# A second batch's first transform stage: sums and differences by GpSimd, all of it ahead of the MLP, with half the products

## The chip, the cores and the metric

The kernel runs on one core of a Trainium2 chip. The metric is the device time of one execution in microseconds (us). A core has five engines that matter here: PE (TensorE, matrix products out of SBUF into PSUM; PEld is its weight load), DVE (VectorE, elementwise work), ACT (ScalarE, elementwise work and copies out of PSUM), POOL (GpSimd, elementwise work within SBUF) and SP (SyncE, which here only issues DMA transfers). Each engine takes the instructions of its queue in order; between engines, semaphores order the work.

## The reference

Eight sequences `x[b]` of 3008 tokens with 256 features are Fourier transformed along the tokens, multiplied by a complex 256 x 256 matrix, biased, soft-thresholded, and transformed back. The result, 24064 tokens, goes through a two-layer MLP of width 2048. All is float32.

```python
X = np.fft.rfft(x, axis=1)
Yr = Xr @ w_r - Xi @ w_i + b_r
Yi = Xr @ w_i + Xi @ w_r + b_i
Yr = np.sign(Yr) * np.maximum(np.abs(Yr) - 0.01, 0.0)
Yi = np.sign(Yi) * np.maximum(np.abs(Yi) - 0.01, 0.0)
y = np.fft.irfft(Yr + 1j * Yi, n=3008, axis=1)
h = y.reshape(24064, 256) @ moe_w_in
out = np.maximum(0.01 * h, h) @ moe_w_out
```

## The kernel before

The length 3008 is split as 47 x 64, so that the transform is a 47-point stage, then a 64-point stage, with no twiddle factors between. The host only reorders the rows of x: for each of 24 frequencies of the 47-point stage it lays out the rows n and 47 - n as two arrays, called here xa and xb, each of 120 partitions.

**First stage, `fwd(b)`.** Of each batch seven column blocks c (six of 512 columns, the last, c = 6, of 256) are loaded (`load`, line 222). Since the 47-point transform of a real sequence needs xa + xb for its cosine part and xa - xb for its sine part, the first batch (b = 0) forms both on DVE (`fold`, line 240) and multiplies the sum by the cosine matrix `fa0` and the difference by the sine matrix `fa1`. Batches 2 to 7 do the same with `fold` on GpSimd, beside the MLP. The second batch (b = 1) is different: `stage_a1` (line 271) takes xa and xb as they are, and for each of the two parts h adds two products, xa by `fa{h}` and xb by `fa0` (cosine) or `fa2` (sine), where `fa2` is `fa1` times -1, made once at line 680. ACT copies each result out of PSUM (line 280) over the input, and SP stores it into a DRAM buffer, `u_dram` (line 281).

**Middle stage, `mid(b)`.** For each of 12 frequency pairs j: load u from `u_dram` (line 329), the 64-point stage (`stage_b`, line 343), the product with the complex matrix (`proj`, lines 375 and following: three real products; DVE adds at line 388, thresholds at 391 and 392; ACT writes the scaled result `zf` at 396 and 400), and the 64-point stage back (`stage_g`, line 414), whose result is stored to `v_dram`. For the first batch all this runs before the MLP, in plain float32, beside the conversion of `w_in` (`convert_win`, lines 131 to 172) from int64 views of float64 into pairs of reduced float32 numbers (`hi`, `lo`) on ACT and DVE. For later batches it is threaded between the MLP's steps.

**Last stage and MLP.** `v_load` (line 459) and `inverse` (line 480) make 470 columns of y at a time; `forms` (lines 505 to 513) makes the seven operands of a Strassen product; then the MLP runs over 47 chunks of 512 tokens with eight steps q each: `moe_a` and `moe_b` (products at line 92, elementwise work at 542 to 563), `moe_o` (line 576). The second weight is converted one piece per step beside the first chunk (`load_wout`, lines 186 to 202).

**Order.** The program is issued in the order of the main part (lines 648 to 739), and a planner that keeps its own times for each instruction then orders the queue of each engine; `tc.issue_after` keeps an instruction from being placed ahead of another one. The second batch's `fwd(1)` is the stream `fp`: its seven loads are issued between steps 5 and 11 of the first middle stage (line 702), `fp.to(0.69)` (line 706) issues `stage_a1` for blocks 0, 1, 2, 3 and 6, and the blocks 4 and 5 are issued inside the MLP loop at its steps 2 and 4 (line 726). `stage_a1` is held behind the eleventh `stage_g` (line 276).

**Buffers.** Tiles share slots by tag. The second batch's inputs `xin` take the tags yc, yc, gf, gh, yl, yh, gh (line 214), which the MLP's own tiles use afterwards. In PSUM, the blocks 4 and 5 use tag psf, the others psh; the MLP's output products use pso.

Of the kernel before, what the change touches and what calls it, by code (L numbers as in the profile page):

```python
# [8 lines left out]
F32 = mybir.dt.float32  # L9
# [12 lines left out]
PA = NK1 * NG  # L22
# [8 lines left out]
def spectral_mlp_kernel(  # L31
# [18 lines left out]
    D = w_r.shape[0]  # L50
# [13 lines left out]
    sb = ctx.enter_context(tc.tile_pool(name="sb", bufs=2))  # L64
# [4 lines left out]
    def bank(tag, bufs):  # L69
        return ps.tile([P, 512], F32, name=tag, tag=tag, bufs=bufs)  # L70

    def products(dst, pairs):

        terms = []
        for l, r in pairs:
            terms += [(l[0], r[0]), (l[0], r[1]), (l[1], r[0])] if len(l) == 2 else [(l[0], r[0])]
        for i, (a, b) in enumerate(terms):
            last = nc.tensor.matmul(dst, a, b, start=(i == 0), stop=(i == len(terms) - 1))  # L78
        return last
# [18 lines left out]
    consts = {}  # L98
# [117 lines left out]
    def fwd(b):  # L216
# [5 lines left out]
        def load(c):  # L222
            cols = slice(2 * c * D, min(2 * c + 2, NS) * D)
            n = cols.stop - cols.start
            if b < NPRE:
                tag, bufs = (XT, XT1)[b][c]
                x2 = sb.tile([PA, 2, 2 * D], F32, name="xin", tag=tag, bufs=bufs)
                x_t[c] = [x2[:, h, :n] for h in range(2)]
            else:
                x_t[c] = [  # L230
                    sb.tile([PA, 2 * D], F32, name=f"xin{h}", tag="uv"[h], bufs=3 - h)[:, :n] for h in range(2)
                ]
            for h, t in enumerate(x_t[c]):
                if b == 0:
                    (act if h else sync).dma_start(t, x[b, h, :, cols])
                else:
                    with tc.issue_after(reads[-1].ins):
                        sync.dma_start(t, x[b, h, :, cols])
# [19 lines left out]
        def stage_a(c, h):  # L258
# [9 lines left out]
            if b == 0:  # L268
                written.append(st)

        def stage_a1(c):

            n = x_t[c][0].shape[1]
            pas = [(bank("psf", 2) if c in (4, 5) else bank("psh", 4))[:PA, :n] for _ in range(2)]
            for h in range(2):
                with tc.issue_after(turning[NPAIR - 2].ins):
                    products(pas[h], [
                        (consts[f"fa{h}32"], (x_t[c][0],)), (consts[f"fa{2 * h}32"], (x_t[c][1],))])
            for h in range(2):
                act.copy(x_t[c][h], pas[h])  # L280
                sync.dma_start(uv[h, :, 2 * c * D:2 * c * D + n], x_t[c][h])

        if b == 1:
            for c in range(NX):
                load(c)
                yield 0
            for c in (0, 1, 2, 3, 6, 4, 5):
                stage_a1(c)
                yield 6 * x_t[c][0].shape[1]
            return  # L290
# [354 lines left out]
    FWD = NS * 6 * D  # L645


    fa32 = sb.tile([PA, 3, PA], F32, name="fa32", tag="xi", bufs=1)
    for h in range(2):
        sync.dma_start(fa32[:, h], fa[h])  # L650
    for h in range(3):
# [25 lines left out]
    act.copy(bz[:1], brow[:1])  # L677
    act.copy(bz[32:33], brow[32:33])
    dve.tensor_sub(bz[32:33], brow[32:33], bz[32:33].bitcast(F32))
    act.mul(fa32[:, 2], fa32[:, 1], -1.0)  # L680
    convert_win(0)
    with tc.issue_after(turned[0].ins):
        split_consts()
# [19 lines left out]
        if i == 13:  # L703
            next(wout)
    m0.finish()
    fp.to(0.69)
    for p in due[0]:
        v_load(p)
    for eh in range(NH):
# [133 lines left out]
```

## Time and profile before

| | |
|---|---|
| median of 3 runs | 2600.41 us (2598.28 to 2602.9) |
| profiled execution, own time | 2600.34 us |
| its span, first to last instruction | 2598.6 us |
| PE busy | 2537.5 us, 98% of the span |
| DVE busy | 1897.1 us, 73% |
| ACT busy | 1668.5 us, 64% |
| POOL busy | 229.6 us, 9% |

All times within the span count from its start. A table by stretches has a row for each: its bounds, its length, and for each engine the busy time in it and, as (x..), how many instructions; then the clock that PE was granted as a share of full speed, the mean busy share of the 16 DMA engines, and the GB/s they moved. A timeline row has start, length, engine, line, operation, what it writes and reads, shapes, and how many in a row are merged (x4); in brackets is the engine's idle time just before, and what ended it. A row of a group has the number of instructions, their busy time, the mean in ns, and the idle time before them. A row "min/median/max" gives the lengths of one in ns. Engine names with a q (SPq) are the engine's sequencer, which issues DMA transfers. The last row of the page's DMA part gives the size of one transfer in KB and the median us from issue to landing.

### The profile page before, as it was taken

Reading aid. Unit: us, or ns where it says so; the run is one execution under the profiler, and the core shown is the slowest. Engines: PE = TensorE matmul, PEld = TensorE weight load, DVE = VectorE, ACT = ScalarE, POOL = GpSimd, SP = SyncE. Lnnn points to the kernel's source line nnn. Section 1 sums busy time; section 2 is a strip of 40 time slices with the busy share of each in tenths; the row PEclk is TensorE's granted clock in tenths of the full one; section 3 lists DMA queues with packets and bytes.
Section 4 is the critical chain, followed back from the end, with each engine's and each line's share of the span. In section 5 each row is a group of like instructions: output and inputs, shape, how many; then the busy total and the mean of one; then the engine's idle time right before and its main releaser. Section 6 shows DMA issues by size and latency. Waiting matters only on the chain.

```text
span 2598.6 us, 42643 instructions
## 1 busy us (share of the span) xinstructions
PE 2537.5 (98%) x16300; PEld 2281.5 (88%) x16300; DVE 1897.1 (73%) x3403; ACT 1668.5 (64%) x3174; POOL 229.6 (9%) x180
## 2 busy tenths in 40 slices
PE   5999999999999999999999999999999999999999
PEld 4689888999889998899988999889998889999998
DVE  7687786776777778777786777877777777767675
ACT  5766665776556666567665666566666667655564
POOL 0001121100110001100021000210002000000000
PEclk8999999999999999999999999999999999999999
DMA  8621132111221113211132111321113221101000
GB/s 259 179 85 50 48 89 72 54 47 48 82 78 49 45 41 90 75 55 51 33 97 68 49 49 37 104 67 49 49 36 101 64 58 48 44 17 32 9 17 17
DMA packets 119912, 165.13 MB, mean 64 GB/s; under 512 B 13601, under 2 KB 69917, under 8 KB 119709
## 3 DMA queue, kind: packets, MB, share of 16 engines
q1 hardware_dynamic: 79120, 115.55, 14.6%
q10 hardware_dynamic: 40589, 46.87, 7.1%
q8 instruction: 128, 2.10, 0.4%
q14 instruction: 75, 0.61, 0.1%
HBM read 86.60 MB, written 75.76 MB: 62 GB/s over the span
## 4 chain that ended last, share of the span: by engine, by line
PE 89%; DVE 3%; DMA 2%; ACT 1%; issue 0%; ACTq 0%; SPq 0%; DVEq 0%
PE pso L576 38%; PE psh L92 34%; PE psf L78 11%; PE psf L480 3%; PE psf L343 3%; DMA u<-u_dram 1%; DMA u_dram<-xin 1%; DVE yl L506 0%; DVE gl L563 0%; DMA raw<-w_out_dram 0%; DVE gf L557 0%; ACT gh L561 0%; DVE yt L511 0%; ACT gf L559 0%; DVE yc L512 0%
## 5 line engine op out<-in xcount | busy, mean ns | idle before, releaser
L92 PE MATMUL psh<-yh,win_hi 128*128 128x256 f32 x2632 | 752.3, 286 | 13.8 <-DVE gf L546 10.6
L92 PE MATMUL psh<-yl,win_hi 128*128 128x256 f32 x2632 | 738.3, 280 | 0.6 <-DVE yl L506 0.5
L92 PE MATMUL psh<-yh,win_lo 128*128 128x256 f32 x2632 | 737.9, 280 | 0.0
L576 PE MATMUL pso<-gh,wout_hi 128*128 128x512 f32 x1504 | 593.9, 395 | 0.0
L576 PE MATMUL pso<-gl,wout_hi 128*128 128x512 f32 x1504 | 591.1, 393 | 0.5 <-DVE gl L563 0.5
L576 PE MATMUL pso<-gh,wout_lo 128*128 128x512 f32 x1504 | 590.4, 393 | 0.0
L563 DVE TENSOR_TENSOR gl<-gf,gh 128x1024 fp32r<-128x1024 f32 x376 | 471.8, 1255 | 92.7 <-ACT gh L561 90.6
L92 PEld LDWEIGHTS psh<-yh,win_hi 128*128 128x128 f32 x2632 | 497.0, 189 | 30.7 <-DVE gf L546 15.4
L92 PEld LDWEIGHTS psh<-yl,win_hi 128*128 128x128 f32 x2632 | 497.0, 189 | 12.5 <-DVE yl L506 1.0
L92 PEld LDWEIGHTS psh<-yh,win_lo 128*128 128x128 f32 x2632 | 496.6, 189 | 0.2
L557 DVE TENSOR_TENSOR gf<-psh,u 128x512 f32<-128x512 f32 x376 | 259.1, 689 | 256.3 <-PE psh L92 255.1
L561 ACT CAST gh<-gf 128x1024 fp32r<-128x1024 f32 x376 | 396.4, 1054 | 7.1
L559 ACT ACTIVATE gf<-gf 128x768 f32<-128x768 f32 x376 | 320.0, 851 | 49.5 <-DVE gf L557 47.7
L576 PEld LDWEIGHTS pso<-gl,wout_hi 128*128 128x128 f32 x1504 | 282.5, 188 | 62.9 <-DVE gl L563 1.0
L576 PEld LDWEIGHTS pso<-gh,wout_hi 128*128 128x128 f32 x1504 | 283.1, 188 | 46.9 <-ACT gh L561 0.4
L576 PEld LDWEIGHTS pso<-gh,wout_lo 128*128 128x128 f32 x1504 | 282.9, 188 | 44.9
L556 ACT ACTIVATE gf<-psh 128x256 f32<-128x256 f32 x376 | 145.5, 387 | 266.6 <-PE psh L92 246.9
L542 ACT COPY p<-psh 128x256 f32<-128x256 f32 x376 | 140.1, 373 | 220.2 <-PE psh L92 219.1
L379 POOL TENSOR_TENSOR kb<-bias,kc 128x512 f32<-128x512 f32 x84 | 119.0, 1417 | 1530.6 <-ACT kc L376 1409.6
L543 DVE TENSOR_TENSOR u<-psh,p 128x256 f32<-128x256 f32 x376 | 158.6, 422 | 105.8 <-ACT p L542 103.5
L545 DVE TENSOR_TENSOR gf<-psh,u 128x256 f32<-128x256 f32 x376 | 159.3, 424 | 29.7 <-PE psh L92 2.0
L546 DVE TENSOR_TENSOR gf<-psh,gf 128x256 f32<-128x256 f32 x376 | 159.1, 423 | 9.0
(134 smaller groups left out, 3253.2 us busy)
## 6 DMA issues: line engine op xcount, KB each, us to landing
u<-u_dram SPq DMA_DIRECT2D x192, 128.0 KB, 2.7
v_dram<-v ACTq DMA_DIRECT2D x192, 128.0 KB, 2.4
out_dram<-ob SPq DMA_DIRECT2D x94, 256.0 KB, 2.1
vin<-v_dram SPq DMA_DIRECT2D x96, 240.0 KB, 3.5
xin<-x_dram SPq DMA_DIRECT2D x90, 240.0 KB, 3.0
u_dram<-xin ACTq DMA_DIRECT2D x72, 240.0 KB, 2.4
u_dram<-xin SPq DMA_DIRECT2D x24, 240.0 KB, 3.9
raw<-w_out_dram SPq DMA_DIRECT2D x8, 512.0 KB, 5.0
```

The source lines that it names most:

```text
L78: last = nc.tensor.matmul(dst, a, b, start=(i == 0), stop=(i == len(terms) - 1))
L92: mlp[:] = [nc.tensor.matmul(dst, a, b, start=start and i == 0, stop=i == 2, skip_group_check=True)]
L542: act.copy(p1, b1[:, lo])
L543: dve.tensor_add(u2, b1[:, hi], p1)
L545: dve.tensor_add(g[:, 3], b2[:, hi], u2)
L546: dve.tensor_add(g[:, 3], b2[:, lo], g[:, 3])
L556: act.activation(g[:, 0], b1[:, lo], AF.Prelu, alpha=SLOPE)
L557: dve.tensor_add(g[:, 1:3], b2.rearrange("p (k n) -> p k n", k=2), u2.unsqueeze(1).broadcast_to([P, 2, HT]))
L559: act.activation(g[:, 1:4], g[:, 1:4], AF.Prelu, alpha=SLOPE)
L561: cp = act.copy(gh, g)
L563: parted[:] = [cp, dve.tensor_sub(gl, g, gh.bitcast(F32))]
L576: mlp[:] = [nc.tensor.matmul(po, a[:, f, s], r[:, i], start=(f == 0 and j == 0), stop=(f == NF - 1 and j == 2),)]
```

## The change

1. `fold1(c)` is new: for the second batch, GpSimd adds and subtracts xa and xb of each block. The sum goes to a spare half tile, the difference over xa. The first spare is a third part of block 4's tile, which is made that much larger; after each block its xb becomes the spare of the next one, in the order 0, 1, 2, 3, 6, 4, 5.
2. `stage_a1` then needs one product for each part instead of two: the sum by `fa0`, the difference by `fa1`. The third matrix `fa2` and the ACT instruction that made it go.
3. The blocks 4 and 5 are no longer held back for the MLP loop: `fp.finish()` issues all folds and all seven blocks ahead of it. In PSUM they use the tag pso instead of psf.

```diff
             if b < NPRE:
                 tag, bufs = (XT, XT1)[b][c]
-                x2 = sb.tile([PA, 2, 2 * D], F32, name="xin", tag=tag, bufs=bufs)
+                spare = b == 1 and c == 4
+                x2 = sb.tile([PA, 3 if spare else 2, 2 * D], F32, name="xin", tag=tag, bufs=bufs)
                 x_t[c] = [x2[:, h, :n] for h in range(2)]
+                if b == 1:
+                    s_t[c] = x2[:, 1]
+                if spare:
+                    s_t[-1] = x2[:, 2]
...
+        def fold1(c):
+
+            xa, xb = x_t[c]
+            n = xa.shape[1]
+            xs = s_t[-1][:, :n]
+            s_t[-1] = s_t.pop(c)
+            pool.tensor_add(xs, xa, xb)
+            pool.tensor_sub(xa, xa, xb)
+            x_t[c] = [xs, xa]
+
         def stage_a1(c):
 
             n = x_t[c][0].shape[1]
-            pas = [(bank("psf", 2) if c in (4, 5) else bank("psh", 4))[:PA, :n] for _ in range(2)]
+            pas = [(bank("pso", 2) if c in (4, 5) else bank("psh", 4))[:PA, :n] for _ in range(2)]
             for h in range(2):
                 with tc.issue_after(turning[NPAIR - 2].ins):
-                    products(pas[h], [
-                        (consts[f"fa{h}32"], (x_t[c][0],)), (consts[f"fa{2 * h}32"], (x_t[c][1],))])
+                    products(pas[h], [(consts[f"fa{h}32"], (x_t[c][h],))])
...
             for c in range(NX):
                 load(c)
                 yield 0
+            for c in (0, 1, 2, 3, 6, 4, 5):
+                fold1(c)
             for c in (0, 1, 2, 3, 6, 4, 5):
                 stage_a1(c)
...
-    fa32 = sb.tile([PA, 3, PA], F32, name="fa32", tag="xi", bufs=1)
+    fa32 = sb.tile([PA, 2, PA], F32, name="fa32", tag="xi", bufs=1)
...
-    act.mul(fa32[:, 2], fa32[:, 1], -1.0)
...
     m0.finish()
-    fp.to(0.69)
+    fp.finish()
...
-        if i in (2, 4):
-            with tc.issue_after(parted[0].ins), tc.issue_after(parted[1].ins):
-                next(fp.gen)
```

More of the change, by code (lines that the diff above doesn't have):

```diff
@@ L645, in spectral_mlp_kernel @@
     FWD = NS * 6 * D
-    fa32 = sb.tile([PA, 3, PA], F32, name="fa32", tag="xi", bufs=1)
+    fa32 = sb.tile([PA, 2, PA], F32, name="fa32", tag="xi", bufs=1)
     for h in range(2):
         sync.dma_start(fa32[:, h], fa[h])
-    for h in range(3):
+    for h in range(2):
         consts[f"fa{h}32"] = (fa32[:, h],)
```

## The prediction

> **What bounds the kernel now.** I read the share of each engine and the chain that ended last first, then a table by stretches of the first 200 us, because every line of the change acts before 150 us.
>
> ```profile
> PE 2537.5 (98%) x16300; PEld 2281.5 (88%) x16300; DVE 1897.1 (73%) x3403; ACT 1668.5 (64%) x3174; POOL 229.6 (9%) x180
> PE 89%; DVE 3%; DMA 2%; ACT 1%; issue 0%; ACTq 0%; SPq 0%; DVEq 0%
> ```
>
> ```profile
> core 0: us, PE busy (x) PEld busy (x) DVE busy (x) ACT busy (x) POOL busy (x), PEclk, DMA share, GB/s
> 58.00:65.00 7.00, 6.36 (x35) 4.93 (x34) 6.87 (x15) 6.46 (x13) 0.00 (x0) 1.00 0.83 266
> 65.00:76.00 11.00, 10.56 (x54) 8.18 (x53) 9.22 (x15) 10.23 (x21) 0.00 (x0) 1.00 0.96 278
> 76.00:85.00 9.00, 9.00 (x48) 7.35 (x47) 8.04 (x17) 7.94 (x18) 0.00 (x0) 1.00 0.52 160
> 85.00:93.00 8.00, 8.00 (x44) 6.65 (x43) 5.09 (x8) 7.74 (x16) 0.00 (x0) 1.00 0.27 66
> 93.00:104.50 11.50, 7.91 (x28) 4.63 (x27) 4.93 (x9) 6.84 (x16) 0.30 (x1) 0.97 0.37 88
> 104.50:116.00 11.50, 11.50 (x31) 5.46 (x30) 6.64 (x12) 4.30 (x7) 0.00 (x0) 0.88 0.73 199
> 116.00:129.00 13.00, 12.87 (x55) 7.87 (x54) 6.83 (x17) 10.81 (x25) 0.00 (x0) 1.00 0.77 239
> 129.00:149.50 20.50, 17.91 (x95) 13.98 (x94) 18.59 (x36) 12.04 (x23) 0.00 (x0) 0.92 0.41 120
> 149.50:168.50 19.00, 16.73 (x106) 14.74 (x104) 18.87 (x41) 15.21 (x32) 0.00 (x0) 1.00 0.33 99
> 168.50:200.00 31.50, 31.44 (x208) 28.86 (x209) 24.43 (x45) 19.83 (x36) 2.58 (x2) 1.00 0.17 51
> ```
>
> Over the whole span TensorE is the chain (89%). From 168.5 us on it is full (31.44 of 31.50), so there a microsecond of start is a microsecond of end. The change, however, sits earlier. From 58 to 93 us the first batch's middle stage runs, with PE, ACT and DVE all near full; GpSimd has nothing to do. From 93 to 104.5 us that stage drains. From 104.5 to 129 us come the second batch's first stage and the first inverse transform. From 129 to 168.5 us DVE is the bound (18.59 of 20.50, 18.87 of 19.00): it converts w_out beside the first MLP chunk.
>
> **What the halved products save on TensorE.** The second batch's first stage (stage_a1) issues for each of seven column blocks four products, each of which the trace shows as two records.
>
> ```profile
> L78 PE MATMUL psh<-xin,fa 120*120 120x512 f32 x32 | 15.9, 640 | 0.0
> L78 PE MATMUL psf<-xin,fa 120*120 120x512 f32 x16 | 7.5, 612 | 0.1
> L78 PE MATMUL psh<-xin,fa 120*120 120x256 f32 x8 | 1.9, 379 | 0.0
> ...
> 119.49 1.88 PE L78 MATMUL psh<-xin,fa 120*120 120x512 f32 x4
> 121.20 0.38 PE L480 MATMUL psf<-ga,vin 120*128 120x128 f32 x2
> ```
>
> The durations overlap, so I go by starts: four records of 512 columns take 121.20 - 119.49 = 1.71 us, 0.43 each, and one of 256 columns half of that. In all 48 x 0.43 + 8 x 0.215 = 22.2 us, and the change leaves half: **11.1 us less work for TensorE**. That is the most that the products can give. Where it falls decides what is seen of it. The x16 row is the last two blocks, which now run inside the MLP (6.8 us): one block before 129 us, where PE would else wait for the first forms, and one after it, where DVE is the bound. The other five blocks (32 x 0.43 + 8 x 0.215 = 15.4 us) run ahead of the MLP. With all seven there, at half, they need 11.1, so PE is through with this stretch **at most 4.3 us earlier**.
>
> Does that start the MLP earlier? Between the inverse transform and the first MLP product stand ACT copies, and ACT serves its queue in order:
>
> ```profile
> 116.04 0.67 ACT L131 ACTIVATE cvq<-raw 128x512 f32<-128x512 uint32 x1 [3.33 <-DMA raw<-w_out_dram]
> L280 ACT COPY xin<-psh 120x512 f32<-120x512 f32 (+1 forms) x7 | 3.5, 521 | 0.0
> 149.09 0.41 ACT L505 CAST yh<-yc 128x256 fp32r<-128x256 f32 x1 [2.32 <-DMA u_dram<-xin]
> ```
>
> ACT stood 3.33 us until 116.04 us for a piece of w_out, and then worked 10.81 of the 13 us to 129, seven copies of stage_a1 among them. The last two blocks' four copies (3.5 / 7, so some 0.5 to 0.6 us each, 2.3 us) now join this side of the MLP; some can move into the time before ACT's wait, since products come twice as fast. Bounds for the start of the MLP: 2.3 us later, if all four copies queue behind 116 us, to 4.3 us earlier. ACT is nearly full after its wait, so I take only a third of PE's lead: **1.5 us earlier**.
>
> Inside the MLP the change removes four copies, four stores and a wait: ACT stood 2.32 us at 149.09 because the slot of the first block of the next chunk was free only once the last second-batch block had been stored. All of DVE's idle time from 129 to 149.5 us is 20.50 - 18.59 = 1.9 us; the 6.8 us of PE there were covered by DVE. So this is worth 0 to 1.9 us; since the row names the wait that goes, I take **1.6**. The scaled matrix (act.mul at line 680) that also goes is one small ACT instruction in the load phase, where ACT waits for products: nothing.
>
> **What the sums and differences cost.** Fourteen GpSimd instructions are added. Later batches do the same on GpSimd, so their price has rows; the times at which the inputs are asked for are in the SP queue.
>
> ```profile
> L245 POOL TENSOR_TENSOR xs<-xin,xin 120x512 f32<-120x512 f32 x36 | 48.1, 1337 | 316.3 <-DVE xz L255 168.8 <-DMA xin<-x_dram 43.9 <-DMA vin<-v_dram 26.2
> L245 POOL TENSOR_TENSOR xs<-xin,xin 120x256 f32<-120x256 f32 x6 | 4.4, 735 | 53.1 <-DVE xz L255 53.1
> ```
>
> ```profile
> 54.60 1.12 SPq L238 DMA_DIRECT2D xin<-x_dram  x2
> 68.92 1.95 SPq L238 DMA_DIRECT2D xin<-x_dram  x4
> 81.67 1.06 SPq L238 DMA_DIRECT2D xin<-x_dram  x2
> xin<-x_dram SPq DMA_DIRECT2D x90, 240.0 KB, 3.0
> ```
>
> With 3.0 us to land, block 0 can be folded from about 58.5 us, block 3 from 73, and block 6, on which the last two wait by the order of the loop, from 85.4. GpSimd is free, so its own time is hidden: done by some 93 us, products from 104.5 us. What is not hidden is what it does to DVE:
>
> ```profile
> 664.57 2.00 POOL L245 TENSOR_TENSOR xs<-xin,xin 120x512 f32<-120x512 f32 x1 [9.65 <-DMA xin<-x_dram]
> 666.64 1.33 POOL L246 TENSOR_TENSOR xin<-xin,xin 120x512 f32<-120x512 f32 x1
> 665.32 1.52 DVE L511 TENSOR_TENSOR yt<-yc,yt 128x256 f32<-128x256 f32 x1
> 666.77 1.49 DVE L512 TENSOR_TENSOR yc<-yc 128x256 f32<-128x256 f32 x1
> L511 DVE TENSOR_TENSOR yt<-yc,yt x47: 412/420/1521, 127.1 to 2519.7; 128x256 f32<-128x256 f32 x47
> 406.99 1.29 POOL L245 TENSOR_TENSOR xs<-xin,xin 120x512 f32<-120x512 f32 x1 [7.39 <-DVE xz L255]
> 407.44 0.69 DVE L557 TENSOR_TENSOR gf<-psh,u 128x512 f32<-128x512 f32 x1 [0.52 <-PE psh L92]
> L254 DVE CAST xz<-xs x42: 286/424/1358, 365.5 to 2029.5; 120x512 fp32r<-120x512 f32 x36, 120x256 fp32r<-120x256 f32 x6
> ```
>
> Two DVE instructions that normally take 0.42 us (median of the x47 row) took 1.52 and 1.49: each ended 0.2 to 0.3 us after the GpSimd instruction beside it had ended. They take turns: DVE, GpSimd, DVE, GpSimd. L557, whose input is in PSUM, keeps its 0.69 us beside GpSimd. L254, a copy with one SBUF input at twice the pace per element, is stretched too (0.42 to 1.36). So a GpSimd fold stops DVE for its own undisturbed time, 1.30 us (the 406.99 row; the mean of 1.337 holds waits of its own; 0.73 for the narrow block), whenever DVE's next instruction reads SBUF only: twelve at 1.30 and two at 0.73 are **17.1 us**. What can take the blow is DVE's idle time and its work out of PSUM:
>
> ```profile
> L388 DVE TENSOR_TENSOR t<-psf,kc 128x512 f32<-128x512 f32 x8 | 5.5, 690 | 1.2 <-ACT kc L376 0.9
> ...
> 70.85 1.13 PE L78 MATMUL psh<-zf,w 128*128 128x512 f32 x2 [0.41 <-ACT zf L400]
> 103.26 1.48 PE L78 MATMUL psh<-zf,w 128*128 128x512 f32 x2 [2.60 <-ACT zf L396]
> ```
>
> From 58 to 93 us DVE is busy 6.87 + 9.22 + 8.04 + 5.09 = 29.2 of 35 us, 5.5 of them L388 out of PSUM. That leaves 23.7 us which exclude GpSimd; 23.7 + 17.1 = 40.8 us do not go into 35. Bounds: if the folds always fell into the 5.8 us idle, the 5.5 us of L388 and the 6.6 us idle from 93 to 104.5 us (17.9 in all), **0**; if each stopped the chain in full, **17.1**. For the value I go stretch by stretch. Eight folds (blocks 0 to 3, 10.4 us) fall into 58 to 76 us, where DVE idles 1.9 us and has about 2.4 us of L388 (four of the eight): DVE falls behind by some 6 us. What is late next: t (L392), then its scaled copy zf on ACT, then stage_g's product on PE, which already waits 0.41 us for zf at 70.85, so there is no slack to speak of; behind it in PE's order stand the next block's products, and ACT is 16.69 of 18 us busy. I let 5 of the 6 reach PE. The other six folds (6.7 us) start at 85.4 us, where DVE idles 2.9 of 8 us; 2 to 3 us of delay, of which I let 2 reach the end, because the drain after 93 us is one chain of DVE, ACT and PE (PE waits 2.60 us for zf at 103.26) and passes on what it gets. Sum **7 us later**, near the capacity excess of 5.8.
>
> The Trainium skill, page "SBUF — State Buffer", section "Who interferes with whom", has the rule: a VectorE instruction with two SBUF inputs, or one in a two-port mode, and a GpSimd instruction that reads SBUF exclude each other, and the second to issue "fully blocks until the first finishes". The trace agrees (0.42 became 1.52). By that rule alone, with DVE always asking, the kernel would come out at 2600.3 + 17.1 - 3.1 = 2614.3 us, an estimate.
>
> **Moved things at no cost.** The loads of x stay where they are. The fourteen stores leave SP's queue before the MLP instead of ten; behind them stand the next inverse's loads, which are needed only for the second chunk. If two stores slip ahead of the first inverse's loads, these come later by two transfers; that lies in the 2.3 us bound above. The last two blocks change their PSUM banks from psf to pso, empty from the last kc copy to the first output product. Slots of yc, gf, gh are now held by the neighbour block too, whose sum lies there, but all stores end before their next user. The clock: 0.92 over 129 to 149.5 us is 1.6 us lost in a half-clock spell there; it may go, stay or double (-1.6 to +1.6), and I take 0.
>
> **Sum**, against the profiled execution's own 2600.34 us (span 2598.6 and 1.7 around it; the median of the runs is 2600.41): 2600.3 + 7.0 - 1.5 - 1.6 = **2604.2 us**.
>
> **Rivals.**
> (a) TensorE is what counts, and the folds find DVE's gaps. For it: 98% PE, and 17.9 us of room on DVE. Against it: the room does not lie where the folds fall, and DVE and ACT are the bound around the removed products. Time: 2600.3 - 11.1 = 2589.2; with the two gains at their upper ends alone (4.3 + 1.9), 2594.1.
> (b) Slower for certain: the turns between GpSimd and DVE in the middle stage, 58 to 104 us, reach the end but for what DVE's idle time in 65 to 93 us takes (1.8 + 1.0 + 2.9 = 5.7), 17.1 - 5.7 = 11.4 us, and ACT's four extra copies eat the earlier start. 2600.3 + 11.4 - 1.6 = 2610.1. It decides from a lock price of 3.1 + 5.2 = 8.3 us, where the two gains no longer keep the loss within what can be measured. For it: three engines full at once and no slack at zf. Against it: GpSimd waits its turn as well.
> (c) The folds do not run as the data land but after the middle stage, for instance behind the memset that is GpSimd's one instruction in the row 93 to 104.5. Then they meet a DVE with more gaps; 17.1 us from the middle of that stretch, some 97 us, end at 114, about when PE reaches the last block (104.5 + 5 x 1.71 + 0.86 = 113.9), so nothing waits: 2600.3 - 3.1 = 2597.2. Against it: nothing else is in GpSimd's queue before them.
>
> **How the numbers follow.** A measurement of this kernel tells about 0.2% (5.2 us) from no change: faster is below 2595.2, slower above 2605.6. Forecast 0.38, with a lock price of 4 to 10 us: its own range 2601 to 2607, 0.32 of it within the 0.2% and 0.06 above. (a) 0.18, faster. (b) 0.30, slower. (c) 0.14, of which 0.02 faster. Faster 0.20, same 0.44, slower 0.36. The range goes from 2594, the upper ends of (a)'s two gains, to 2612, just past (b).
>
> **What would show it.** Lock: GpSimd busy in 58 to 95 us, and L392, L391, L348 or L172 there with means over 1 us; the last stage_g product starting near 110 us instead of 103.3. If it starts at 103 to 104, (a) or (c) holds. Start of the MLP: from that product to the point where DVE becomes full (the row border of 129 us), 25.7 us before; 23 to 25 after. MLP: no wait of yh for a store; DVE still full until the w_out pieces are done. The forecast falls if DVE's instructions keep their lengths beside GpSimd, or if the middle stage gives back what it loses before 104 us.

## The result, and the profile after

The changed kernel takes **2631.61 us** (median of 4 runs, 2629.91 to 2635.54) against 2601.65 us for the kernel before on the same chip (2598.28 to 2606.91): a ratio of 1.0115, 95% interval 1.0094 to 1.0137. It is 30.0 us slower, where 2604.2 was forecast. Two executions at a lower granted clock, one of the kernel before (3133.82 us) and one of a_gate_late45_s32 (3579.09 us), are left out of all ratios and ranges below, and of the latter's median.

From the page of the changed kernel, the busy times and the chain of waits, as they were shown of before:

```profile
PE 2551.8 (97%) x16272; PEld 2299.3 (87%) x16272; DVE 1908.1 (73%) x3403; ACT 1665.1 (63%) x3173; POOL 251.8 (10%) x194
PE 89%; DVE 4%; DMA 3%; ACT 2%; issue 1%; SPq 0%; ACTq 0%; DVEq 0%
```

TensorE is still the chain, but it is busy 14.3 us *longer* (2551.8 against 2537.5), although 14 products, 11.1 us by the prediction, were taken away. GpSimd is busy 22 us longer.

The table by stretches of the changed kernel, same columns and borders as before:

```profile
core 0: us, PE busy (x) PEld busy (x) DVE busy (x) ACT busy (x) POOL busy (x), PEclk, DMA share, GB/s
65.00:76.00 11.00, 9.87 (x50) 7.31 (x48) 10.86 (x14) 8.93 (x17) 7.31 (x5) 1.00 0.93 269
76.00:85.00 9.00, 6.00 (x20) 4.89 (x21) 9.00 (x13) 4.34 (x10) 2.58 (x2) 0.81 0.39 108
...
93.00:104.50 11.50, 10.56 (x51) 8.20 (x50) 7.66 (x8) 7.96 (x18) 6.84 (x6) 1.00 0.21 46
104.50:116.00 11.50, 8.44 (x22) 3.53 (x21) 5.18 (x10) 7.85 (x17) 0.30 (x1) 1.00 0.50 122
116.00:129.00 13.00, 9.82 (x35) 5.33 (x34) 7.97 (x15) 7.57 (x15) 0.00 (x0) 0.94 0.86 281
129.00:149.50 20.50, 11.05 (x58) 10.47 (x57) 15.15 (x37) 13.01 (x30) 0.00 (x0) 0.67 0.50 161
149.50:168.50 19.00, 14.84 (x73) 13.09 (x72) 16.99 (x33) 11.11 (x18) 0.00 (x0) 0.77 0.18 56
168.50:200.00 31.50, 29.76 (x196) 26.89 (x194) 26.32 (x50) 19.63 (x38) 1.29 (x1) 1.00 0.21 59
```

Three things differ. From 65 to 85 us DVE is full (10.86 of 11.00, 9.00 of 9.00) with GpSimd beside it, and PE falls from 9.00 to 6.00 in 76 to 85 us. From 129 to 168.5 us PE is busy 25.89 of 39.5 us instead of 34.64, DVE no longer is the bound (15.15 of 20.50), and the granted clock is 0.67 and 0.77 instead of 0.92 and 1.00. And from 168.5 to 200 us PE is not quite full yet (29.76).

How the delay grows is read at three marks of ACT: the copy of the last stage_g product (start of the row), the thirteenth gh of the MLP, and the end of the span. First before, then after:

```profile
104.78 0.59 ACT L418 COPY v<-psh 128x512 f32<-128x512 f32 x1 [1.57 <-PE psh L78]
222.72 1.05 ACT L561 CAST gh<-gf 128x1024 fp32r<-128x1024 f32 x1
```

```profile
113.98 0.58 ACT L434 COPY v<-psh 128x512 f32<-128x512 f32 x1 [0.20 <-PE psh L78]
237.84 1.05 ACT L577 CAST gh<-gf 128x1024 fp32r<-128x1024 f32 x1
```

The middle stage ends 9.2 us later; the thirteenth gh comes 15.1 us later; the end 29.5 us later (spans of 2628.1 and 2598.6). Of the 9.2 us, 0.5 are there already at the stage's first such copy (61.17 against 60.69 us). So 8.7 us arise in the middle stage, 5.9 between it and the steady part of the MLP, and **14.4 us in the steady part**, of which the prediction says only that a microsecond of start is a microsecond of end.

The steady part: page rows of the MLP's products (L92 in both kernels), before and after.

```profile
L92 PE MATMUL psh<-yh,win_hi 128*128 128x256 f32 x2632 | 752.3, 286 | 13.8 <-DVE gf L546 10.6
L92 PE MATMUL psh<-yl,win_hi 128*128 128x256 f32 x2632 | 738.3, 280 | 0.6 <-DVE yl L506 0.5
```

```profile
L92 PE MATMUL psh<-yh,win_hi 128*128 128x256 f32 x2632 | 758.8, 288 | 19.7 <-DVE gf L562 14.1
L92 PE MATMUL psh<-yl,win_hi 128*128 128x256 f32 x2632 | 745.2, 283 | 0.1
```

The same products, as many of them, at the same clock, each 2 to 3 ns longer. Since they overlap, the distance of their starts is what counts. Near the end of the kernel, where nothing else runs on PE, one run of 21 such products lies between these rows of the timeline (first of the run, first record behind it), before and after:

```profile
2576.49 0.28 PE L92 MATMUL psh<-yh,win_hi 128*128 128x256 f32 x1
2578.94 0.40 PE L576 MATMUL pso<-gh,wout_hi 128*128 128x512 f32 x1
```

```profile
2605.95 0.29 PE L92 MATMUL psh<-yh,win_hi 128*128 128x256 f32 x1
2608.48 0.40 PE L592 MATMUL pso<-gh,wout_hi 128*128 128x512 f32 x1
```

2.45 us / 21 = 116.7 ns before, 2.53 / 21 = 120.5 ns after. Over all neighbouring L92 records after 200 us (distances above 135 ns left out) the mean goes from 117.08 to 119.11 ns; with 7896 such products in a run that is 16.0 us. The products of the output layer are even a little closer (229.97 and 229.54 ns); over the 4512 of them that gives 1.9 us back, which leaves 14.1 of the 14.4 us.

What could slow a product by 2% that the diff doesn't touch? The tile fa32 had three matrices and has two. It stands ahead of most tiles in the memory map of the program: every tile behind it lies 416 bytes lower (yh at byte 162720 of a partition instead of 163136, yl at 84384 instead of 84800, as the built programs list them), while the weights win_hi and win_lo lie ahead of it and stay (7712, 36384). It is 416 and not the matrix's 480, because the tile xi shares the slot and keeps 1024 bytes of it.

The middle stage: two groups of VectorE's instructions from 58 to 93 us in the kernel before, then VectorE and GpSimd in the changed kernel, from the timeline.

```profile
L392 DVE TENSOR_TENSOR t<-t,c 128x512 f32<-128x512 f32 x9 | 6.2, 690 | 0.0
L348 DVE TENSOR_TENSOR ef<-ef 128x256 f32<-128x256 f32 x7 | 3.0, 424 | 1.7 <-ACT ef L347 1.7
```

```profile
67.49 1.32 DVE L364 TENSOR_TENSOR ef<-ef 128x256 f32<-128x256 f32 x1
68.74 2.30 DVE L172 TENSOR_TENSOR win_lo<-ws,win_hi 128x1024 fp32r<-128x1024 f32 x1
70.96 1.75 DVE L133 TENSOR_SCALAR cva<-cva 128x1024 f32<-128x1024 f32 x1
75.78 1.75 DVE L408 TENSOR_TENSOR t<-t,c 128x512 f32<-128x512 f32 x1
```

```profile
67.25 1.28 POOL L282 TENSOR_TENSOR xin<-xin 120x512 f32<-120x512 f32 x1 [3.66 <-DMA u<-u_dram]
70.19 1.97 POOL L282 TENSOR_TENSOR xin<-xin 120x512 f32<-120x512 f32 x1 [0.23 <-DMA xin<-x_dram]
74.89 2.08 POOL L282 TENSOR_TENSOR xin<-xin 120x512 f32<-120x512 f32 x1 [1.05 <-DMA xin<-x_dram]
```

L364, L172, L133 and L408 take 0.42, 1.23, 0.69 and 0.69 us in the kernel before (there L348, L172, L133 and L392). They take turns with the folds, as predicted, and GpSimd pays too: the fourteen folds are busy 21.75 us instead of the 17.1 of undisturbed ones. From the first copy of a stage_g product to the last, twelve of VectorE's instructions are stretched, nine of them by 0.90 to 1.07 us. Against the medians of the same instructions in the kernel before they lose 10.2 us together. L404, whose input is in PSUM, keeps its 0.68 us.

Between the two: the DMA issues on SP's queue and the inverse transform on PE. First before, then after.

```profile
107.90 1.68 SPq L459 DMA_DIRECT2D vin<-v_dram  x4
110.63 14.15 SPq L281 DMA_DIRECT2D u_dram<-xin  x10
124.88 2.13 SPq L459 DMA_DIRECT2D vin<-v_dram  x4
```

```profile
118.67 0.32 SPq L475 DMA_DIRECT2D vin<-v_dram  x1
119.08 0.81 SPq L295 DMA_DIRECT2D u_dram<-xin  x2
...
123.54 0.43 SPq L475 DMA_DIRECT2D vin<-v_dram  x1
...
130.75 1.93 SPq L475 DMA_DIRECT2D vin<-v_dram  x4
```

```profile
131.84 0.28 PE L92 MATMUL psh<-yh,win_lo 128*128 128x256 f32 x1
136.88 3.33 PE L496 MATMUL psf<-ga,vin 120*128 120x128 f32 x14 [4.77 <-DMA vin<-v_dram]
```

Before, the first chunk's four vin loads were issued together ahead of the stores; now they alternate with stores, each of which waits for an ACT copy. And the second chunk's inverse transform, which stands in PE's queue behind the first three MLP products, waits 4.77 us for its own vin, issued only at 130.75 behind the last stores. In the kernel before the products of block 4 ran at that place (3.67 us from 125.59). The clock granted to PE is 0.50 from 127.5 to 130.9, 134.4 to 141.1, 144.6 to 151.3 and 154.9 to 161.6 us; in the kernel before, from 129 to 168.5 us, only from 138.1 to 141.4.

### The profile page after: what moved, and what is told of

The parts are those of the page before. It is cut to its first block, busy times and chain, and to the rows that moved or that the text cites. A ratio compares the mean times of both kernels' runs of the same rounds, so it can differ in the third digit from the quotient of the medians.

```text
span 2628.1 us, 42612 instructions
## 1 busy us (share of the span) xinstructions
PE 2551.8 (97%) x16272; PEld 2299.3 (87%) x16272; DVE 1908.1 (73%) x3403; ACT 1665.1 (63%) x3173; POOL 251.8 (10%) x194
## 3 DMA queue, kind: packets, MB, share of 16 engines
q1 hardware_dynamic: 79120, 115.55, 14.3%
## 4 chain that ended last, share of the span: by engine, by line
PE 89%; DVE 4%; DMA 3%; ACT 2%; issue 1%; SPq 0%; ACTq 0%; DVEq 0%
PE pso L592 37%; PE psh L92 34%; PE psf L78 11%; PE psf L496 3%; PE psf L359 3%; DMA u_dram<-xin 1%; DMA u<-u_dram 1%; DMA xin<-x_dram 0%; DVE yl L522 0%; DVE gl L579 0%; DMA vin<-v_dram 0%; PE psh L78 0%; ACT zf L416 0%; PE pso L78 0%; DMA raw<-w_out_dram 0%
## 5 line engine op out<-in xcount | busy, mean ns | idle before, releaser
L92 PE MATMUL psh<-yh,win_hi 128*128 128x256 f32 x2632 | 758.8, 288 | 19.7 <-DVE gf L562 14.1
L92 PE MATMUL psh<-yh,win_lo 128*128 128x256 f32 x2632 | 746.8, 284 | 0.0
L92 PE MATMUL psh<-yl,win_hi 128*128 128x256 f32 x2632 | 745.2, 283 | 0.1
L92 PEld LDWEIGHTS psh<-yh,win_hi 128*128 128x128 f32 x2632 | 499.8, 190 | 36.9 <-DVE gf L562 19.1
L92 PEld LDWEIGHTS psh<-yl,win_hi 128*128 128x128 f32 x2632 | 499.1, 190 | 11.3 <-DVE yl L522 0.3
L92 PEld LDWEIGHTS psh<-yh,win_lo 128*128 128x128 f32 x2632 | 498.7, 189 | 0.2
```

The source lines that it names most:

```text
L92: mlp[:] = [nc.tensor.matmul(dst, a, b, start=start and i == 0, stop=i == 2, skip_group_check=True)]
```

## Experiments

All are timed against the kernel before on the same chip (its medians 2602.1 to 2602.4). "Old addresses" means the changed kernel with room for the third matrix kept. Five questions.

**1. Is it the place?** a_layout is the changed kernel with old addresses, the third matrix unused; b_shift32 is the kernel *before* with everything behind fa32 32 bytes higher.

```diff
 # a_layout
-    fa32 = sb.tile([PA, 2, PA], F32, name="fa32", tag="xi", bufs=1)
+    fa32 = sb.tile([PA, 3, PA], F32, name="fa32", tag="xi", bufs=1)
 # b_shift32
-    fa32 = sb.tile([PA, 3, PA], F32, name="fa32", tag="xi", bufs=1)
+    fa32 = sb.tile([PA, 3 * PA + 8], F32, name="fa32", tag="xi", bufs=1)[:, :3 * PA].rearrange("p (h k) -> p h k", h=3)
```

> The changed kernel with the matrix tile fa32 made three matrices wide again (the third is not used), so that every tile behind it in SBUF keeps the place it had before the change, 416 bytes further up. Theory 'place': the MLP's first products start every 119 to 120 ns instead of 117 in the changed kernel because of where their operands lie; then the pace here is 117, and the time falls by about 7896 x 2 ns = 16 us, to 2614 to 2618. Rival 'state of the engine' (clock, heat, the order of the work): pace and time stay at 119 and 2630. In both the delay of the middle stage (last stage_g near 113 us) stays, since the folds stay.

Measured: 2616.57 us (2614.93 to 2619.13), ratio 1.0052 (1.0034 to 1.0070), 14.2 above before instead of 30.0. The mean distance of the L92 products is 117.09 ns again (117.08 to 117.10 in the eight other kernels below that have the old addresses). **The place costs 15.8 us**, half of the loss, and has nothing to do with the work that the change moves.

> The kernel before with the tile fa32 made 32 bytes wider and nothing else, so that every tile behind it moves by 32 bytes. Theory 'place', and within it that the place modulo 64 bytes counts (the change moved the tiles by 416 = 6.5 x 64): pace 119 instead of 117 and the time 14 to 18 us above the kernel before, at 2615 to 2620. If only the place counts but not modulo 64: pace and time as before, 2601. Rival 'state of the engine': 2601 too.

Measured: 2595.92 us (2594.66 to 2597.99), ratio 0.9976 (0.9967 to 0.9986): 6.5 us *faster* than before, at 116.94 ns. That the place decides stands; the rule that I had guessed for it falls.

The weights don't move and the moving operands do, so I ordered the kernels by the distance of yh (and of yl, which has the same) from win_hi, as a remainder of 128 bytes, and foretold three more.

```diff
 # b_shift96, b_shift160, b_shift64: the kernel before with
-    fa32 = sb.tile([PA, 3, PA], F32, ...
+    fa32 = sb.tile([PA, 3 * PA + 24], F32, ...      # + 40, + 16
```

> The kernel before with its fa32 tile 96 bytes wider, so that every tile behind it lies 96 bytes higher; nothing else. Distance of the MLP's moving tiles (yh, yl) from the weights (win_hi, win_lo), which do not move, in remainders of 128 bytes: 32 in the kernel before (117 ns from one MLP product to the next), 64 in b_shift32 (113 to 118), 0 in the changed kernel (118.5 to 120). Theory 'remainder of the distance': here it is 0 again, so the pace is 118.5 to 120 ns and the time 2612-2618. Rival 'only large moves or the order of the program matter': 116 to 118 ns and 2596-2604.

> The kernel before with everything behind fa32 160 bytes higher: the remainder of 128 bytes is 64, as in b_shift32, that of 256 bytes is 192. Theory 'remainder of 128': pace as in b_shift32 (means of 116 to 118 ns, some runs of products at 113), 2594-2598. If the period is longer than 128 bytes: any pace, 2598-2616.

> The kernel before with everything behind fa32 64 bytes higher: the remainder of 128 bytes is 96, the one step of 32 that is not yet seen (0: 119 to 120 ns and about 14 us slower; 32: the kernel before; 64: 6 to 7 us faster). If the pace depends on how far the two operands lie apart in that remainder, either way round, 96 is 32 away from 0 like the kernel before: 116.5 to 118 ns, 2599-2605. If not, any pace between those seen: 2594-2616.

```
kernel        shift   remainder   mean distance   time      against its own before
a_layout          0       32        117.09 ns    (its order differs)
before            0       32        117.08       2602.1
after          -416        0        119.11       2631.6     (its order differs)
b_shift96       +96        0        119.11       2616.2     +14.1 (ratio 1.0054, 1.0039 to 1.0069)
b_shift32       +32       64        116.94       2595.9      -6.5 (0.9976, 0.9967 to 0.9986)
b_shift160     +160       64        116.19       2595.1      -7.0 (0.9971, 0.9959 to 0.9982)
b_shift64       +64       96        119.82       2622.6     +20.5 (1.0081, 1.0066 to 1.0096)
```

From the timeline of b_shift96, first and last of one run of 21 products near the end (20 distances, 2.41 us, 120.5 ns as in the changed kernel):

```profile
2570.61 0.29 PE L92 MATMUL psh<-yh,win_hi 128*128 128x256 f32 x1
2573.02 0.29 PE L92 MATMUL psh<-yh,win_lo 128*128 128x256 f32 x1
```

b_shift96 does the same work as the kernel before in the same order and has the pace of the changed kernel, to the hundredth of a nanosecond; the distance times 7896 gives 16.0 us, the output products give 2.0 of them back, and 14.1 were measured. b_shift160 lies with b_shift32. The remainder told these two beforehand. The third, b_shift64, did not come as I had put it: 96 is not like 32, it is the slowest of the four. So equal remainders gave nearly equal paces here, but I have no rule for their order, and 116.94 against 116.19 says that 128 bytes are not the whole of it. For b_shift32 the L92 distances explain 1.1 us and those of the output products (229.3 instead of 230.0 ns, 4512 of them) 3; the other 2 to 3 us are not accounted for.

**2. What do the folds cost, and is it the turns?** Base is a_layout. a_nofold leaves the fourteen sums and differences out, so that the parts of x are multiplied as they are; a_dve gives them to VectorE; a_gate holds them back until pair 10 of the middle stage is through, by a GpSimd copy of one column of that pair's t ahead of them.

```diff
 # a_nofold
-            pool.tensor_add(xs, xa, xb)
-            pool.tensor_sub(xa, xa, xb)
-            x_t[c] = [xs, xa]
+            x_t[c] = [xa, xb]
 # a_dve
-            pool.tensor_add(xs, xa, xb)
-            pool.tensor_sub(xa, xa, xb)
+            dve.tensor_add(xs, xa, xb)
+            dve.tensor_sub(xa, xa, xb)
 # a_gate, in proj, behind the threshold of t
+            if b == 0 and j == 10:
+                gt = sb.tile([P, 2 * NG * NK1], F32, name="odd", tag="odd", bufs=1)
+                gates.append(pool.tensor_copy(gt[:, :1], t[:, 0, :1]))
 # and in fwd
             for c in (0, 1, 2, 3, 6, 4, 5):
-                fold1(c)
+                with tc.issue_after(gates[0].ins):
+                    fold1(c)
```

> The kernel of a_layout with the fourteen sums and differences left out: xa is multiplied by the cosine matrix and xb by the sine matrix as they are. Theory 'turns': the folds hold up VectorE and cost the middle stage 9 us; without them the last stage_g is back at 103 to 104 us and the time falls by 8 to 10 us against a_layout, to 2605 to 2608. Rival 'order': the folds cost little, the loss lies in the order behind the middle stage: the time falls by under 3 us.

Measured: 2607.30 us (2604.93 to 2610.29), ratio 1.0019 (1.0010 to 1.0029): **the folds cost 9.3 us**, though GpSimd had nothing else to do. In the traces the middle stage, from its first v copy to its last, takes 53.7 us in a_layout and 44.1 in a_nofold, as in the kernel before; VectorE's instructions there are stretched by 8.5 us in all in a_layout, by nothing in a_nofold. 4.9 us above before remain, with half the products.

> The kernel of a_layout with the sums and differences on VectorE instead of GpSimd (0.69 us each there). Theory 'turns': what costs is GpSimd's 1.3 us in turn with VectorE while VectorE is full; where the planner puts the folds into VectorE's queue behind the middle stage's work, the last stage_g is within 2 us of 103 and the time 6 to 9 us under a_layout, 2606 to 2610. Rival: any fold before the products costs the same, since VectorE is the engine that is full: 14 x 0.6 = 8 us, time as a_layout.

Measured: 2611.53 us (2610.91 to 2615.53), ratio 1.0040 (1.0026 to 1.0054): 5.0 us below a_layout, a little less than expected, and the two intervals overlap. The gain does not come from where theory 'turns' put it: the last stage_g product starts at 112.22 us, not within 2 us of 103, and the middle stage takes 53.2 us, as long as in a_layout. On VectorE the fourteen folds take 9.0 us (0.65 each) and stretch nothing; on GpSimd they take nothing from VectorE's queue and stretch it by 8.5. In this stage that comes to the same, as the rival said. What makes the 5.0 us isn't shown.

> a_layout with the fourteen sums and differences held back until pair 10 of the first batch's middle stage has been thresholded (GpSimd first copies one column of that t into an unused tile; the folds stand behind that copy in its queue). Theory 'turns' (GpSimd stops VectorE while VectorE, ACT and PE are all full): the last stage_g copy is no longer late, VectorE's instructions from 58 to 90 us have their old lengths, and most of the 9.3 us that a_nofold won comes back: 2607-2610, unless the folds, which then end some 18 us after the gate, hold up the second batch's products; with that, 2611-2614. Rival 'a fold costs its time wherever it falls': 2615-2618.

Measured: 2605.39 us (2603.64 to 2608.63), ratio 1.0017 (1.0007 to 1.0026): **11.2 us below a_layout**, as much as leaving the folds out gave (9.3), within the noise. Groups of VectorE's instructions from 58 to 93 us, the changed kernel and a_gate:

```profile
L408 DVE TENSOR_TENSOR t<-t,c 128x512 f32<-128x512 f32 x7 | 5.8, 830 | 0.0
L364 DVE TENSOR_TENSOR ef<-ef 128x256 f32<-128x256 f32 x6 | 4.5, 744 | 0.9 <-ACT ef L363 0.8
L172 DVE TENSOR_TENSOR win_lo<-ws,win_hi 128x1024 fp32r<-128x1024 f32 x2 | 3.5, 1762 | 1.2 <-ACT win_hi L171 1.2
```

```profile
L409 DVE TENSOR_TENSOR t<-t,c 128x512 f32<-128x512 f32 x8 | 5.5, 685 | 0.0
L365 DVE TENSOR_TENSOR ef<-ef 128x256 f32<-128x256 f32 x7 | 2.9, 418 | 1.7 <-ACT ef L364 1.7
L172 DVE TENSOR_TENSOR win_lo<-ws,win_hi 128x1024 fp32r<-128x1024 f32 x2 | 2.5, 1226 | 1.9 <-ACT win_hi L171 1.9
```

The lengths are the old ones again (830, 744 and 1762 ns go to 685, 418 and 1226). The folds now run from here to here:

```profile
100.34 1.26 POOL L282 TENSOR_TENSOR xin<-xin 120x512 f32<-120x512 f32 x1
117.69 1.33 POOL L283 TENSOR_TENSOR xin<-xin 120x512 f32<-120x512 f32 x1
```

They end at 119.0 us instead of 100.2, and that is the cheaper place. It isn't free: the last pair of the middle stage meets them, four of VectorE's instructions are stretched by 3.8 us together, and PE waits 6.0 us once for its zf.

**3. What are the 4.9 us above before that a_nofold keeps?** a_late45 is a_layout with blocks 4 and 5 back inside the MLP, in psf banks, as before; a_nofold_late45 the same without the folds. a_vin leaves all seven blocks ahead, but issues the first inverse's vin loads ahead of the stores.

```diff
 # a_late45, a_nofold_late45
-            pas = [(bank("pso", 2) if c in (4, 5) else ...
+            pas = [(bank("psf", 2) if c in (4, 5) else ...
-    fp.finish()
+    fp.to(0.69)
 # and again in the loop over moe()
+        if i in (2, 4):
+            with tc.issue_after(parted[0].ins), tc.issue_after(parted[1].ins):
+                next(fp.gen)
 # a_vin
-    fp.finish()
     for p in due[0]:
         v_load(p)
+    fp.finish()
 # and in stage_a1
-                sync.dma_start(uv[h, ...
+                with tc.issue_after(reads[-1].ins):
+                    sync.dma_start(uv[h, ...
```

> a_layout with the last two blocks of the second batch's first stage back inside the MLP, in psf banks, as in the kernel before; the GpSimd sums, the halved products and the old addresses stay. Theory 'order' (having all seven blocks ahead of the MLP lost about 5 us instead of gaining 3): 2610-2613, gh 13 some 17 us behind the last stage_g copy as before. My prediction's own terms (the move ahead of the MLP gains 1.5 and the wait of yh that goes 1.6): the time rises by about 3, to 2619.5. Rival 'neutral': DVE's conversion of w_out decides the end of this stretch either way, 2615-2618.

Measured: 2610.11 us (2605.80 to 2612.02), ratio 1.0031 (1.0020 to 1.0041): 6.5 us below a_layout, where my own terms asked for 3 above it.

> a_nofold (no sums and differences, old addresses, half the products, 2607.3) with the last two blocks back inside the MLP. The fourteen folds are left out: the parts of x are multiplied as they are. It asks where the 4.9 us come from that a_nofold still stood above the kernel before. Theory 'order of the seven blocks' (the stores of all seven blocks stand in SP's queue ahead of the second chunk's vin, PE waits for it, 6.8 us in five waits, and its clock is at half for part of the next 40 us): that wait is gone and the time is 2599-2603. Rival 'halved products and something else in the program': 2605.5-2608.

Measured: 2600.25 us (2598.91 to 2603.45), ratio 0.9992 (0.9982 to 1.0002): 7.0 us below a_nofold. What PE waited for from 104 to 200 us (total, times, longest), the changed kernel, a_nofold, and a_nofold_late45:

```profile
PE psf L496 <- DMA vin<-v_dram: 7.9, 5, 4.8
```

```profile
PE psf L494 <- DMA vin<-v_dram: 6.8, 5, 3.3
```

```profile
PE psh L92 <- ACT yh L519: 3.1, 1, 3.1
PE psf L494 <- DMA vin<-v_dram: 1.2, 2, 0.6
```

**The order of the seven blocks costs 6.5 to 7 us.** With it undone, the wait for vin falls from 6.8 to 1.2 us; the kernel before has none there. But that wait is not all of it: in a_layout PE waits 3.3 us for vin and 4.1 us once for yc, in a_late45 for neither, and no run tells which of the waits makes the loss. What is left of the change then, half the products and nothing for it, is worth 1.8 us, inside what can be told from nothing.

> Base: the changed kernel with the old addresses (a_layout, 2616.6 us). Only the order of SP's queue is changed: the loads of vin for the first inverse transform are issued ahead of the second batch's stores. Theory 'order of the queue' (in the changed kernel vin was issued from 118.7 to 123.5 us, between stores that wait for ACT's copies, where before it was issued at 108 to 109, and the point where the MLP's fourth gh is made came 5 us later behind the last stage_g copy than before): vin lands within 7 us of the last stage_g copy (13.7 in the changed kernel), gh 12 comes 13 to 15 us behind that copy instead of about 4 to 5 us more, and the time falls by 3 to 6 us, to 2610.5-2613.5. Rival 'ACT': vin's place is idle cover, ACT's seven blocks of copies and VectorE's forms set the start of the MLP: vin earlier, the time within 1.5 us of 2616.6.

Measured: 2614.10 us (2612.86 to 2614.53), ratio 1.0047 (1.0030 to 1.0064): 2.5 us below a_layout, just short of the 3 expected, and the two intervals overlap, so this gain can't be told from nothing. The place of the first inverse's loads is the smaller part at most; PE then stood 7.1 us at yh, and the second chunk's inverse still 3.3 us at vin. Which part of the other 4 us is that wait and which the half clock behind it, no run here separates.

**4. Do they add up?**

> Both edits of a_gate and a_vin. If the two costs are separate and both real, they add up: 2602-2606, about the time of the kernel before. If the later folds hold up the stores and with them nothing but the next inverse's loads, the same. If only one of the two is real, the time of that one alone, 2608-2613; if neither, 2615-2618.

Measured: 2603.77 us (2602.14 to 2606.68), ratio 1.0004 (0.9995 to 1.0014): 1.6 below a_gate. This lies in the expected 2602 to 2606, but so does a_gate alone, and 1.6 us can't be told from nothing.

a_gate_late45 is a_gate with the edit of a_late45; a_gate_late45_s32 is that 32 bytes higher.

> The changed kernel at the old addresses, with the folds held back until pair 10 (a_gate, 2605.4) and the last two blocks back inside the MLP (a_late45, 2610.1). Theory 'turns and order are two costs': the folds of those two blocks end at 119 us but are wanted only inside the MLP, so the gains add up in part: 2599-2603, at or below the kernel before. Rival: the order of a_late45 gained only because the folds were in the way, so nothing is added: 2604-2607.

Measured: 2604.41 us (2602.61 to 2605.67), ratio 1.0005 (0.9996 to 1.0014), only 1.0 below a_gate, as the rival said. The two gains do not add. In a_gate PE waits only 1.2 us for vin, so there was little left to win: the two loads that the second chunk's inverse wants are issued at 128.43 us, ahead of the last three stores, and PE works on the last blocks' products until 130.7. That this is the reason is not shown. The rival's own reason, that the order of a_late45 gained only because the folds were in the way, falls with a_nofold_late45, which gains 7.0 us without any folds.

> The same with every tile behind fa32 32 bytes higher, as in b_shift32, which was 6.5 us faster than the kernel before. Theory 'place is a cost of its own, whatever the order': 6 us below a_gate_late45, 2593-2598, below both kernels. Rival: the gain of b_shift32 belongs to its order of work: within 2 us of a_gate_late45.

Measured: 2596.57 us, ratio 0.9979 (0.9969 to 0.9989): 7.8 below a_gate_late45, as b_shift32 was 6.5 below the kernel before. The place is a cost of its own.

The traces say where each cost lies. The profiled executions come to the middle stage at different times (its first v copy starts between 60.7 and 65.9 us), so the lengths of stretches are compared, in us, of one execution each:

```
                   first to last   stretched      last v copy    from there
                   v copy          VectorE work   to 13th gh     to the end
before                 44.1            0.2           117.9         2375.8
changed kernel         52.8           10.2           123.9         2390.3
a_layout               53.7            8.5           123.1         2374.7
a_vin                  53.1            9.4           121.7         2374.7
a_late45               52.0            8.8           116.8         2374.2
a_nofold               44.1           -0.1           122.7         2376.0
a_nofold_late45        44.6              -           116.5         2375.2
a_gate                 47.8            3.8           114.4         2377.9
a_dve                  53.2           -0.3           118.9         2379.2
b_shift96              44.3              -           119.5         2388.2
```

The folds act in the first stretch, and there the stage grows by about what VectorE's instructions are stretched, or in a_dve by the 9.0 us of added work. The order acts in the second: both kernels with the edit late45 are some 6 us shorter there than their bases. The place acts in the last. Why a_gate and a_dve take 2 to 5 us longer there than the others at their addresses is open.

**5. Is there a version that beats both kernels?** Three do, by 0.2 to 0.3%: a_gate_late45_s32 (2596.6), b_shift32 (2595.9) and b_shift160 (2595.1). The best are the kernel before with its tiles moved; the change itself adds nothing to them.

## Why the prediction was wrong, step by step

The 30.0 us, by medians: place 15.8 (after to a_layout), folds 9.3 (a_layout to a_nofold), order 6.7 (a_nofold to a_nofold_late45, each against its own before), products -1.8. The prediction had 0, 7.0, -3.1, and the products' gain within the last. The intervals of the medians are 5 to 9 us wide, so the pieces are not known to the tenth; the stretches in the table above give 15.6, 9.6 and 6.2 for the first three.

- **The place: the step that failed most, and it is one sentence.** "The scaled matrix (act.mul at line 680) that also goes is one small ACT instruction ... nothing." I priced the instruction and not the room that its matrix took. With the tiles 416 bytes lower the MLP's 7896 products run at 119.11 instead of 117.08 ns. "There a microsecond of start is a microsecond of end" was right of the start, and left out that the pace itself can change. No rival had it, so the time lies outside the range.
- **The turns: right in mechanism and place, and nearly in size.** 7.0 was forecast, 9.3 measured, inside the 4 to 10 that I gave the forecast, though above the 8.3 from which rival (b) was to decide. DVE is full from 65 to 85 us, the folds run from 59.6 to 100.2 us, the last stage_g product starts at 112.92 (forecast near 110, before 103.26). The sign that I gave for it was a poor one: L172 is over 1 us in the mean (1.76), but it was that before the change (1.23), and L364 and L408 are not (0.74, 0.83), since only some of theirs meet a fold. The two terms behind 7.0 both missed, in opposite ways. VectorE loses 10.2 us and not 17.1, and GpSimd waits its turn too, 4.7 us in all; and the stage passes on about all of it (it is 8.7 us longer; in a_layout VectorE loses 8.5 and the stage is 9.6 longer), where I let idle time and work out of PSUM take more than half. That 7.0 came so near 9.3 owes something to luck. The Trainium skill, page "SBUF — State Buffer", section "Who interferes with whom", says that issue order decides who blocks; the trace agrees, both sides are stretched here (a fold of 1.28 us became 2.08, an L364 of 0.42 became 1.32).
- **"1.5 us earlier" for the MLP: wrong in sign.** I took PE's lead in the stretch ahead of the MLP as the thing to gain. But PE was not short of time there: in the kernel before, block 4 ran where PE would else stand before the first forms, as the prediction itself says. Moving it ahead put four more copies and stores in front of work that was wanted, and the whole move costs 6.5 to 7 us; that the freed time on PE was of no use to anybody is argued and not shown by a run of its own.
- **"Moved things at no cost": the sentence that failed** is "behind them stand the next inverse's loads, which are needed only for the second chunk". That is true, and PE wants the second chunk's inverse right behind the first three MLP products: the 4.77 us wait. The chance that stores slip ahead of the first inverse's loads was named and put into a bound of 2.3 us; a_vin measures 2.5, not clear of noise. The half clock that follows PE's waits was given 1.6 us either way and taken as 0; the changed kernel's clock is 0.67 and 0.77 where it was 0.92 and 1.00, and some of the 6.7 us may be that. (The Trainium skill, page "TensorE: Matmul & The Clock Gate", part on the clock gate, says that PE falls back to half after an idle window of about 3.4 us. The trace agrees in part: waits of 4.77 and 3.46 us lie in the stretch of 0.67, and the half-clock spells there last 3.4 or 6.8 us. But shorter waits were followed by half clock too: in the kernel before, one of 2.60 us until 103.26 by the spell from 104.0 to 107.2.)
- **"1.6 us" for the wait of yh on a store: the wait did go** (no yh of the changed kernel waits for a store), but DVE was no longer the bound in that stretch (15.15 of 20.50 us, where it had 18.59), so the sum's reason for a gain was gone, and none shows.
- **Rivals.** (a) falls: half the products gain 1.8 us, 4.7 at the end of the interval, and not 11.1. (b) was nearest: its mechanism holds, its price of 11.4 was a little high, and even without the cost of the place (a_layout, 2616.6) the order takes the time past its 2610.1. (c) did not happen, but a_gate makes it happen: 11.2 us better than folds that run as the data land. Its price (2597.2) was too good, as the late folds meet the last pair.

## What to carry to other kernels

Before costing a change by its instructions, compare the memory maps: a tile that shrinks moves every tile behind it, and in a kernel of thousands of equal products a 2% change of pace outweighs what was changed; keep the place with a dummy when comparing, and try a few shifts of 32 bytes when tuning. An idle GpSimd is not free beside a full VectorE: hold such work back to where VectorE has gaps. Giving it to VectorE itself left the stage just as long here. And before moving work ahead, look at what it covered where it stood, and which loads stand behind its stores in the same queue.

## What the runs showed of the hardware

The distance from one 128x256 product to the next, both operands in SBUF, depends on where the operands lie: means of 116.2 to 119.8 ns, single distances mostly of 112 to 125 ns, with the same work. It is reproducible: two kernels with the same addresses but another order of work (before and a_layout) have 117.08 and 117.09 ns, two whose addresses differ by 512 bytes (after and b_shift96) 119.11 both. It is not a matter of what VectorE or ScalarE do meanwhile: in the kernel before, distances in which both engines are idle average 117.2 ns, those in which both are busy 117.1; in the changed kernel 119.4 and 118.9. Within one kernel whole runs of 21 products go at 113 and others at 118 (b_shift32). The pairs of the output layer, whose operands move together, keep 229.3 to 230.0 ns in every kernel. Why, and by which rule, stays open; that it is the distance between the two operands rather than the address of one is how the kernels were ordered, and no run moved the weights alone.
